# Sixteen copies of the conv tap rows in DRAM for the read of the conv band

## Chip, cores and metric

One core of one Trainium2 chip. The metric is the device time of one execution in microseconds (us).

## What is computed

A causal convolution over the sequence with one softmaxed 7-tap filter per head, followed by a two-layer feed-forward block. Cut to what matters:

```python
# x (8, 4096, 192), weight (8, 7), w_in (192, 2048), w_out (2048, 192), all float32
w = softmax(weight, axis=-1)                       # 8 heads, 7 taps
x_pad = concatenate([zeros(B, 6, D), x], axis=1)   # causal padding
out = einsum('hk,bskhg->bshg', w, windows of x_pad)  # 24 channels per head
a = out.reshape(32768, 192)
h = a @ w_in
g = where(h > 0, h, exp(min(h, 0)) - 1)            # ELU
result = g @ w_out                                 # (32768, 192) float32
```

## The kernel before

The 32,768 tokens are cut into 32 super-tiles of 1,024 tokens. A super-tile runs through 16 steps, one for each 128 columns of the hidden layer; steps are numbered n = 0 to 511 over the whole kernel. In each step TensorE (PE) makes the hidden values H of two groups of 512 tokens (`w_in` matmuls, L748), ScalarE (ACT) takes their exponential E (L542), GpSimd (POOL) clips it to at most 1 (L470), VectorE (DVE) combines E and H into the ELU output gT (L609), and PE later multiplies gT with `w_out` into ops (L782), which ACT evicts to osb and SyncE (SP) stores. PE's whole order is written out at build time in the list `steps`; PE works through it in order and waits where an operand or a PSUM bank isn't there.

The convolution of super-tile s is done ahead of its feed-forward, on PE: the band matrix Tm (128 partitions, 8 heads, 128 columns, bf16), which holds the taps of each head along its diagonals, is the stationary operand and the x rows in xg the moving one (L726). ACT evicts the result to csb (L520), and a transposing DMA that SP issues turns it into att, the left operand of the `w_in` matmuls. Super-tile 0 takes another way, through xT and diagonal matrices Dg, so the first matmuls with Tm are those for super-tile 1. `EARLY_CONV` puts them beside steps n = 7 to 10, and those of super-tile 2 at n = 13 and 14. Ahead of its first one, PE waits in this order for the band, for the x rows, and for their zero padding:

```python
if m == 0:
    W(s_band, 48)
...
for part in range(2):
    x_ready(W, s, part)
```

How Tm is made: SP issues three DMAs, all on its own queue, after the small weight load and one load of x rows (xf). The first (L799) writes zero rows from the zeroed tile zw to the DRAM tensor conv_taps, the second (L804) writes the eight heads' tap rows from zt (128 elements each, the softmaxed taps at columns 6 to 12), and the third (L809) reads the band back. Before the second SP waits for zt (`W(s_wp, 1)`), before the third for both writes (`W(s_band, 32)`). In conv_taps a copy of the taps is ten rows of 128: a zero row, eight heads, a zero row. Partition p of Tm reads eight rows' worth of elements from a start that moves one element back per partition, so each partition gets the taps shifted by one: 1,024 elements, 2,048 bytes, in one run. With two copies, the outer dimension of that read is 2 and the next one 64.

Beside these, POOL issues the big loads of the beginning, one after the other, each with a cast from float32: the six pieces of `w_in` (L424), the two halves of xg for super-tile 1 (L397), `w_out` (L454) and the two halves of xg for super-tile 2 (L397). They all move through the same DMA engines as SP's transfers. SP's next issue after the band is the first transpose.

Of the kernel before, what the change touches and what calls it, by code (L numbers as in the profile page):

```python
# [8 lines left out]
BF16 = mybir.dt.bfloat16  # L9
# [3 lines left out]
P = 128  # L13
HP = 64
FC = 128
D = 192
HEADS = 8
KSIZE = 7
CPH = 24
CW = 128  # L20
# [4 lines left out]
TAP = 6  # L25
# [16 lines left out]
CONV_AT = ((0, 1, 1, 0), (4, 1, 1, 1), (9, 2, 0, 0), (12, 2, 0, 1))  # L42
EARLY_CONV = ((7, 1, 0, 0), (8, 1, 0, 1), (9, 1, 1, 0), (10, 1, 1, 1), (13, 2, 0, 0), (14, 2, 0, 1))
OPS_CONV = 2
FIRST = {}
M_NS, R_NS, C_NS = 215.8, 82.5, 102.5
QUAD = 4
# [6 lines left out]
def bass_lightweight_conv__then__act_elu_kernel(  # L54
# [28 lines left out]
    def take_bank(what):  # L83
        k = len(prior)
        prior.append(occupant[k % 6])
        occupant[k % 6] = what
        turn_of[what] = k % 6
# [4 lines left out]
    for t in range(NS):  # L92
        for half, stretches in enumerate(ROUNDS):
            n, at = NQ * (t + 1) + LAG + 8 * half, [0, 0]
            if t == 0 and half in FIRST:
                n, stretches = FIRST[half]
            for turned, sizes in stretches:
# [35 lines left out]
    def acc_of(op):  # L133
        t, half, q, kb, turned = op[1]
        return (t, half, kb if (t, half) == (last, 1) else 0, op[3])
# [48 lines left out]
    for x_, op in enumerate(steps):  # L184
        if op[0] in "hc" and not any(op[3:]):
            if op[0] == "h" or op[1] >= OPS_CONV:
                take_bank(op[:3])
# [27 lines left out]
            t, half = divmod(n_half - 1, 2)  # L215
            previous[n_half // 2, n_half % 2, 0, g] = (t, half, 0, g)

    taps = nc.dram_tensor("conv_taps", (2 * (HEADS + 2) * CW,), BF16).ap()

    xb = nc.dram_tensor("x_cast", (NT, D), BF16).ap()  # L220

    with ExitStack() as stack:
        def sbuf(name, shape, dt):
            return stack.enter_context(nc.sbuf_tensor(name, shape, dt))
# [28 lines left out]
        zt = sbuf("zt", [HEADS, CW], BF16)  # L253
        xf = sbuf("xf", [P, 2, QUAD, D], FP32)
        zw = sbuf("zw", [P, GS], BF16)
# [76 lines left out]
        def bank_of(what):  # L332
            if what[0] == "c" and what[1] < OPS_CONV:
                return ops[:, what[2], :]
            k = turn_of[what]
            return H[:, k // 2, GS * (k % 2) : GS * (k % 2 + 1)]

        def load_first(eng, k):
            eng.dma_start(
                xf[:, k, :, :].rearrange("p i d -> p (i d)"),  # L340
                x_flat[GS * k : GS * (k + 1), :].rearrange("(p i) d -> p (i d)", i=QUAD),
            ).then_inc(s_xl[k], 16)

        def conv_read(W, m):
            W(s_ce, 2 * (m + 1))

        def out_group(eng, t, half, g, kb=None):
            b = (2 * t + half) % 2
            row = SUP * t + GS * g + 2 * P * half
            if kb is not None:  # L350
                eng.dma_start(
                    out[row + P * kb : row + P * (kb + 1), :], osb[:, b, g, kb, :]
                ).then_inc(s_out[b], 16)
                return
            dst = out[row : row + 2 * P, :].rearrange("(k p) d -> p k d", p=P)
            if t == 0:
                dst = bass.AP(
                    tensor=out.tensor,
                    offset=(GS * half + 1 - g) * D,
                    ap=[[QUAD * D, P], [2 * D, 2], [1, D]],  # L360
                )
            eng.dma_start(dst, osb[:, b, g, :, :]).then_inc(s_out[b], 16)
# [5 lines left out]
        def taken(W, acc):  # L368
            W(s_od if acc in on_dve else s_oev, place[acc] + 1)
# [16 lines left out]
        def turn_att(eng, s):  # L386
            eng.dma_start_transpose(
                out=att[:, s % 2, :, :].rearrange("p j (w t) -> p (j w) t", t=TOK),
                in_=csb[0:TOK, s % 2, :],
            ).then_inc(s_att[s % 2], 16)  # L390
# [228 lines left out]
        def _tensor(pe):  # L619
# [4 lines left out]
            def wait_bank():  # L624
                was = prior[turns[0]]
                turns[0] += 1
                if was is None:
                    return
                if was[0] == "h":
                    W(s_tt, 2 * was[1] + was[2] + 1)  # L630
                else:
                    W(s_ce, 2 * was[1] + was[2] + 1)
# [62 lines left out]
            for x_, op in enumerate(steps):  # L695
# [10 lines left out]
                elif op[0] == "c":  # L706
# [5 lines left out]
                    elif hh == 0:  # L712
# [6 lines left out]
                        W(s_z, z_need[s])  # L719
                        if m >= OPS_CONV:  # L720
                            wait_bank()
# [40 lines left out]
                else:  # L762
# [6 lines left out]
                    if x_ in begins:  # L769
# [4 lines left out]
                        else:  # L774
                            W(s_ce, 2 * (OPS_CONV - 1) + g + 1)
                    elif steps[seen[acc]][2] != rt:
# [16 lines left out]
        @block.sync  # L793
        def _sync(sy):
            W = Waits(sy)
            sy.dma_start(wh[:], weight[:, :]).then_inc(s_wd, 16)
            load_first(sy, 1)
            W(s_zw, 1)
            sy.dma_start(  # L799
                bass.AP(tensor=taps.tensor, offset=0, ap=[[(HEADS + 2) * CW, 2], [(HEADS + 1) * CW, 2], [1, CW]]),  # L800
                zw[0:2, 0 : 2 * CW].rearrange("p (a e) -> p a e", a=2),
            ).then_inc(s_band, 16)
            W(s_wp, 1)
            sy.dma_start(  # L804
                bass.AP(tensor=taps.tensor, offset=CW, ap=[[CW, HEADS], [(HEADS + 2) * CW, 2], [1, CW]]),
                zt[:, :].unsqueeze(1).to_broadcast([HEADS, 2, CW]),
            ).then_inc(s_band, 16)
            W(s_band, 32)
            sy.dma_start(  # L809
                Tm[:, :, :].rearrange("p h e -> p (h e)"),  # L810
                bass.AP(tensor=taps.tensor, offset=CW + TAP + KSIZE - 1, ap=[[(HEADS + 2) * CW - HP, 2], [-1, HP], [1, HEADS * CW]]),
            ).then_inc(s_band, 16)

            def load_cast(s):
                W(s_cv, 4 * (s - NXB))
                W(s_xb[s % 2], 16 * ((s - 1) // 2 + (s % 2)))
                if s > NXB + 1:
                    W(s_xb[(s - 1) % 2], 16 * ((s - 2) // 2 + ((s - 1) % 2)))
                for part in range(2):
                    row = s * SUP + GS * part - PAD  # L820
                    for w0, w1, rows in ((0, WPG - 1, P), (WPG - 1, WPG, GS - TOK * (WPG - 1) + PAD)):
                        v0 = WPG * part
                        sy.dma_start(
                            xg[0:rows, s % NXB, v0 + w0 : v0 + w1, :],
                            bass.AP(
                                tensor=xb.tensor,
                                offset=(row + TOK * w0) * D,
                                ap=[[D, rows], [TOK * D, w1 - w0], [1, D]],
                            ),
                        ).then_inc(s_xq[s % NXB][part], 16)  # L830

            for x_, op in enumerate(steps):
                if op[0] == "h" and op[2:] == (0, 0):
                    s, i = divmod(op[1], NQ)
                    if i == X_LOAD and s and s + 3 < NS:
                        load_cast(s + 3)
                    if op[1] == X_LATE[1]:
                        load_cast(3)
                elif op[0] == "c" and op[3:] == (1, HB - 1):
                    m, b = op[1:3]  # L840
                    s = m // 2 + 1
                    if m % 2 and b:
                        conv_read(W, m)
                        for u in range(2):
                            W(s_h[u], NQ * (s - 1))
                        turn_att(sy, s)
                elif x_ in stops:
                    acc = acc_of(op)
                    t, half, kb, g = acc
                    if (t, half) == (last, 1):  # L850
                        if (kb, g) != (1, 1):
                            taken(W, acc)
                            out_group(sy, t, half, g, kb)
                    else:
                        taken(W, acc)
                        out_group(sy, t, half, g)
            for b in range(2):
                sy.wait_ge(s_out[b], 32 * NS + 32 * b)
# [28 lines left out]
```

## Time and profile before

| what | value |
|---|---|
| median of 3 runs | 730.81 us (730.28 to 730.85) |
| the profiled execution's own time | 730.68 us |
| its span | 728.6 us |
| granted TensorE clock, mean | 0.995 |
| DMA packets | 129,883, 69.12 MB |
| SP's hardware queue (q1) | 123,592 packets, 30.3% of 16 engines' span |
| POOL's software queue (q0) | 5,872 packets, 14.8% |
| band read Tm<-conv_taps | one issue, 256 KB, at 5.68 us |

The span runs from the first to the last instruction of the profiled execution; its own time has some 2 us more around it. Times in the trace count from the span's start. A "wait" names the engine that stood idle, the line it stood before, and what came last. The chain follows the work that ended last backwards, at each step to what released it. The granted clock is the share of TensorE's full speed; 0.50 is half speed.

### The profile page before, as it was taken

To read this page: it belongs to the slowest core of one execution; us is meant where nothing else is said; L and a number is where in the kernel's file an instruction comes from. 1 tells how busy PE (TensorE), PEld (TensorE's weight loads), DVE (VectorE), ACT (ScalarE), POOL (GpSimd) and SP (SyncE) were. 2 spreads that over 40 slices of the span, in tenths; PEclk is the share of its full clock that TensorE was granted. 3 is DMA by queue.
4 is the path that set the end of the run, shared out by engine and by line. 5 is a ranking of instruction groups with operands and counts; after the bars stand their busy time and mean duration, and the time that the engine had idled before them with its cause. 6 is when DMAs were issued, how large, how long until landed. Compare 5 with 4: busy or idle time off the path is not lost.

```text
span 728.6 us, 28723 instructions
## 1 busy us (share of the span) xinstructions
PE 715.9 (98%) x11866; PEld 620.9 (85%) x11866; DVE 651.0 (89%) x1043; ACT 656.0 (90%) x1286; POOL 631.0 (87%) x1078
## 2 busy tenths in 40 slices
PE   8699999999999999999999999999999999999997
PEld 4398888888888888888888888888888888888897
DVE  5599999999999999999999999999999999999994
ACT  6699999999999999999999999999999999999993
POOL 8588888898888898888898888898888898888893
PEclk9899999999999999999999999999999999999999
DMA  9655335455435544335455445355446454532212
GB/s 176 105 102 115 71 93 117 95 91 99 86 95 115 91 94 107 79 93 116 90 95 99 86 95 115 87 99 97 85 97 116 80 105 95 92 93 70 59 35 67
DMA packets 129883, 69.12 MB, mean 95 GB/s; under 512 B 93960, under 2 KB 128520, under 8 KB 129288
## 3 DMA queue, kind: packets, MB, share of 16 engines
q1 hardware_dynamic: 123592, 52.04, 30.3%
q0 software_dynamic: 5872, 14.75, 14.8%
q8 instruction: 93, 1.52, 0.9%
q10 hardware_dynamic: 288, 0.49, 0.2%
q14 instruction: 38, 0.31, 0.1%
HBM read 43.51 MB, written 36.58 MB: 110 GB/s over the span
## 4 chain that ended last, share of the span: by engine, by line
PE 95%; DMA 2%; POOL 1%; ACT 0%; DVE 0%; issue 0%; ACTq 0%
PE ops L782 51%; PE H L748 40%; PE H L726 3%; DMA xg<-in_x_dram 2%; PE H L782 1%; POOL w_in L424 1%; POOL E L470 0%; DVE gT L609 0%; ACT E L542 0%; PE ops L726 0%; POOL xg L397 0%; ACT csb L520 0%; POOL x_cast L413 0%; POOL x_cast L416 0%; POOL sel L439 0%
## 5 line engine op out<-in xcount | busy, mean ns | idle before, releaser
L609 DVE SCALAR_TENSOR_TENSOR gT<-E,H 128x512 f16<-128x512 f32 x1024 | 645.2, 682 | 63.3 <-POOL E L470 56.0
L470 POOL TENSOR_SCALAR E<-E 128x512 f32<-128x512 f32 x1024 | 606.1, 616 | 85.2 <-ACT E L542 81.1
L542 ACT ACTIVATE E<-H 128x512 f32<-128x512 f32 x1024 | 565.0, 611 | 55.5 <-PE H L748 50.7
L748 PE MATMUL H<-att,w_in 64*128 64x512 bf16 x3072 | 604.9, 378 | 1.3 <-DVE gT L609 1.1
L782 PE MATMUL ops<-w_out,gT 64*128 64x192 f16 x8064 | 587.0, 243 | 0.0
L782 PEld LDWEIGHTS ops<-w_out,gT 64*128 64x128 f16 x8064 | 516.4, 94 | 54.5 <-PE ops L782 29.4
L748 PEld LDWEIGHTS H<-att,w_in 64*128 64x128 bf16 x3072 | 258.9, 94 | 20.8 <-DVE gT L609 6.5
L726 PE MATMUL H<-xg,Tm 64*128 64x240 bf16 x480 | 87.6, 263 | 0.3 <-DVE gT L609 0.3
L520 ACT ACTIVATE csb<-H 128x480 bf16<-128x480 f32 x120 | 70.7, 589 | 0.0
L512 ACT ACTIVATE osb<-ops 128x384 f32<-128x384 f32 x125 | 61.0, 488 | 7.3 <-PE ops L782 5.7
L726 PEld LDWEIGHTS H<-xg,Tm 64*128 64x128 bf16 x480 | 38.2, 93 | 16.2 <-issue 0.6
L416 POOL DMA_DIRECT2D x_cast<-in_x_dram x29 | 15.6, 538 | 0.0
L726 PE MATMUL ops<-xg,Tm 64*128 64x240 bf16 x16 | 4.3, 362 | 5.4 <-DMA xg<-in_x_dram 5.4
L726 PEld LDWEIGHTS ops<-xg,Tm 64*128 64x128 bf16 x16 | 1.6, 114 | 7.3 <-issue 5.9
L782 PE MATMUL H<-w_out,gT 64*128 64x192 f16 x128 | 6.4, 243 | 0.0
L782 PEld LDWEIGHTS H<-w_out,gT 64*128 64x128 f16 x128 | 5.7, 94 | 0.0
L637 PE MATMUL ops<-zw 128*128 128x512 bf16 x9 | 3.6, 579 | 1.3 <-DVE zw L552 1.3
L601 DVE COPY osb<-ops 128x384 f32<-128x384 f32 x1 | 0.6, 558 | 4.3 <-PE ops L782 4.3
L698 PE MATMUL ops<-zw 64*128 64x512 bf16 x12 | 4.4, 377 | 0.0
L424 POOL DMA_DIRECT2D w_in<-in_moe_w_in_dram x6 | 3.9, 662 | 0.2 <-DMA wh<-in_weight_dram 0.2
L637 PEld LDWEIGHTS ops<-zw 128*128 128x128 bf16 x9 | 1.2, 141 | 3.2 <-issue 1.9
L397 POOL DMA_DIRECT2D xg<-in_x_dram x4 | 3.5, 878 | 0.0
(49 smaller groups left out, 28.0 us busy)
## 6 DMA issues: line engine op xcount, KB each, us to landing
out_dram<-osb SPq DMA_DIRECT2D x126, 192.0 KB, 3.3
x_cast<-in_x_dram POOLq DMA_DIRECT2D x29, 384.0 KB, 5.3
xg<-x_cast SPq DMA_DIRECT2D x58, 192.0 KB
xg<-x_cast SPq DMA_DIRECT2D x58, 26.2 KB
xg<-in_x_dram POOLq DMA_DIRECT2D x4, 240.0 KB, 17.6
w_in<-in_moe_w_in_dram POOLq DMA_DIRECT2D x2, 384.0 KB, 9.9
w_out<-in_moe_w_out_dram POOLq DMA_DIRECT2D x1, 768.0 KB, 18.9
w_in<-in_moe_w_in_dram POOLq DMA_DIRECT2D x2, 288.0 KB, 6.4
```

Source lines behind the costliest of these rows:

```text
L416: g.dma_start(xb[s * SUP : (s + 1) * SUP, :].rearrange("(p t) d -> p (t d)", p=P), x_flat[s * SUP : (s + 1) * SUP, :].rearrange("(p t) d - ...
L424: g.dma_start(w_in[HP * r : HP * (r + 1), :, c0:c1], moe_w_in.rearrange("(p j) f -> p j f", j=3)[:, :, c0:c1],).then_inc(s_w[k], 16)
L470: g.tensor_scalar(out=E[:, n % NE, u, :], in0=E[:, n % NE, u, :], scalar1=1.0, scalar2=0.0, op0=ALU.min, op1=ALU.max,).then_inc(s_clp)
L512: a.activation(*out_pieces(acc), ACT.Copy).then_inc(s_oev)
L520: return a.activation(csb[:, s % 2, :].rearrange("p (j v h i) -> p h j v i", j=3, v=2 * WPG, h=HEADS)[:, h0 : h0 + HB], bank_of(("c", m, b ...
L542: a.activation(E[:, n % NE, u, :], bank_of(op[:3]), ACT.Exp).then_inc(s_exp)
L609: v.scalar_tensor_tensor(out=gT[:, s % NG3, q, u, :], in0=E[:, n % NE, u, :], scalar=1.0, in1=bank_of(op[:3]), op0=ALU.subtract, op1=ALU.m ...
L637: pe.matmul(ops[:, 0, :], zw[:, 0:P], zw[:], start=True, stop=True)
L698: pe.matmul(ops[:, 1 - rt, :], zw[HP * rt : HP * (rt + 1), 0:P], zw[HP * rt : HP * (rt + 1), :], start=True, stop=True, tile_position=(HP ...
L726: ins = pe.matmul(bank_of(op[:3])[:, n1 * hh : n1 * (hh + 1)], Tm[HP * rt : HP * (rt + 1), h, :], xg[HP * rt : HP * (rt + 1), s % NXB, :, ...
L748: ins = pe.matmul(bank_of(op[:3]), w_in[HP * r : HP * (r + 1), j, RUN * FC * (q // RUN) + q % RUN : RUN * FC * (q // RUN + 1) : RUN,], att ...
L782: ins = pe.matmul(to[:, d0 : d0 + D], gT[HP * rt : HP * (rt + 1), t % NG3, q, g, t0 : t0 + P], w_out[HP * rt : HP * (rt + 1), q, :], start ...
```

## The change

conv_taps gets sixteen copies of the ten rows instead of two. The zero write covers sixteen copies (from sixteen partitions of zw), the tap write repeats each head's row sixteen times, and the band read's outer dimension becomes 16 with 8 partitions each. The elements that each partition of Tm receives are the same.

```diff
+BANDS = 16
...
-    taps = nc.dram_tensor("conv_taps", (2 * (HEADS + 2) * CW,), BF16).ap()
+    taps = nc.dram_tensor("conv_taps", (BANDS * (HEADS + 2) * CW,), BF16).ap()
...
             sy.dma_start(
-                bass.AP(tensor=taps.tensor, offset=0, ap=[[(HEADS + 2) * CW, 2], [(HEADS + 1) * CW, 2], [1, CW]]),
-                zw[0:2, 0 : 2 * CW].rearrange("p (a e) -> p a e", a=2),
+                bass.AP(tensor=taps.tensor, offset=0, ap=[[(HEADS + 2) * CW, BANDS], [(HEADS + 1) * CW, 2], [1, CW]]),
+                zw[0:BANDS, 0 : 2 * CW].rearrange("p (a e) -> p a e", a=2),
             ).then_inc(s_band, 16)
             W(s_wp, 1)
             sy.dma_start(
-                bass.AP(tensor=taps.tensor, offset=CW, ap=[[CW, HEADS], [(HEADS + 2) * CW, 2], [1, CW]]),
-                zt[:, :].unsqueeze(1).to_broadcast([HEADS, 2, CW]),
+                bass.AP(tensor=taps.tensor, offset=CW, ap=[[CW, HEADS], [(HEADS + 2) * CW, BANDS], [1, CW]]),
+                zt[:, :].unsqueeze(1).to_broadcast([HEADS, BANDS, CW]),
             ).then_inc(s_band, 16)
             W(s_band, 32)
             sy.dma_start(
                 Tm[:, :, :].rearrange("p h e -> p (h e)"),
-                bass.AP(tensor=taps.tensor, offset=CW + TAP + KSIZE - 1, ap=[[(HEADS + 2) * CW - HP, 2], [-1, HP], [1, HEADS * CW]]),
+                bass.AP(tensor=taps.tensor, offset=CW + TAP + KSIZE - 1, ap=[[(HEADS + 2) * CW - P // BANDS, BANDS], [-1, P // BANDS], [1, HEADS * CW]]),
             ).then_inc(s_band, 16)
```

## The prediction

> **What bounds the kernel now.** I read the page's engine rows first, then the TensorE waits of the stage around the conv band, then the chain, then stretches of that stage, then the trace's landing records of the DMAs involved.
>
> The page first. PE is busy 98% of the span and the chain that ended last is 95% PE:
>
> ```profile
> PE 715.9 (98%) x11866; PEld 620.9 (85%) x11866; DVE 651.0 (89%) x1043; ACT 656.0 (90%) x1286; POOL 631.0 (87%) x1078
> PE 95%; DMA 2%; POOL 1%; ACT 0%; DVE 0%; issue 0%; ACTq 0%
> ```
>
> So PE leaves 728.6 - 715.9 = 12.7 us idle in all, and a few DMA transfers can only matter inside that. The DMA share of the chain, 2%, is one piece. The waits between 17 and 30 us, longest first (engine, line, waited-for: total, times, longest), and the chain in order of time (start, us, what):
>
> ```profile
> POOL E L470 <- ACT E L542: 7.2, 3, 5.9
> ACT E L542 <- PE H L748: 6.8, 3, 6.1
> DVE gT L609 <- POOL E L470: 6.7, 3, 5.6
> PEld ops L726 <- issue: 5.9, 2, 5.6
> PE ops L726 <- DMA xg<-in_x_dram: 5.4, 1, 5.4
> ```
> ```profile
> 7.29 15.86 DMA xg<-in_x_dram
> 23.15 0.14 issue
> 23.28 0.35 PE ops L726
> ```
>
> The reader is to see one stall. At step n = 7 PE reaches the first conv matmul (L726). It waits 5.36 us, until 23.28; ACT, POOL and DVE run dry behind it. The last thing to come was the second half of the x rows of super-tile 1 (an xg load that POOL issued at 7.29 and that landed at 23.15). From 40 us on PE has no idle at all, so what is saved up to there should reach the end.
>
> Now the stage in stretches (columns: busy PE, PEld, DVE, ACT, POOL, then granted clock, DMA share, GB/s):
>
> ```profile
> 17.90:21.30 3.40, 0.03 (x1) 0.00 (x0) 2.57 (x5) 0.78 (x2) 1.59 (x3) 1.00 1.34 215
> 21.30:23.30 2.00, 0.02 (x2) 0.05 (x3) 0.00 (x0) 0.00 (x0) 0.00 (x0) 0.51 1.45 177
> 23.30:28.20 4.90, 4.84 (x30) 2.79 (x30) 1.46 (x3) 3.06 (x6) 2.02 (x4) 0.50 0.26 35
> 28.20:32.60 4.40, 3.61 (x27) 1.25 (x24) 3.70 (x7) 4.28 (x10) 3.42 (x7) 1.00 0.04 5
> ```
>
> The DMA engines are saturated during the wait, and the clock is at half (0.50) for 4.9 us after it: the stall is paid twice.
>
> Why does that xg load land so late? By the landing records, fourteen of its sixteen increments came between 16.67 and 18.39 us (mean 17.32), the other two at 22.74 and 23.15. The earlier half shows the same: fourteen by 17.09, two at 21.30 and 21.75. The band's read (Tm from conv_taps, L809, issued at 5.68) has just two data landings, at 21.55 and 22.02, and its 128 packets of 2,048 B run from 11.06 to 21.5 us as two interleaved trains. **Two DMA engines carry the whole band, and the x rows that share these two engines come 4 to 5 us after the rest.** Even without the xg wait, the band itself would hold PE until 22.02.
>
> **What the Trainium skill says.** "DMA: Bandwidth & Descriptors", section "Why a DMA increments its semaphore by 16 and not by 1": an SP-issued DMA runs on the largest k up to 16 that divides the slowest dimension of both sides; only those k engines post a landing and the sequencer writes the other 16 - k. The trace agrees: the band's semaphore shows three early increments (2.13, 4.07, 6.76, each some 0.4 to 1.1 us after an issue), ten landings (5.00 to 5.66: two for the zero rows, eight for the tap rows) and the last two of the read. Same page, section "Queues, rings and completion order": an engine serves its queues in turn, a packet each. The trace agrees from 11.06 us on, when a band packet comes every 0.245 us on each of the two engines beside w_in packets and later every 0.12 us beside xg packets; it doesn't show it for the 5.4 us between the issue and the first packet, in which only earlier POOL transfers ran. "TensorE: Matmul & The Clock Gate", section "Part 1: The HAM clock gate (the "warmup" mystery)": the clock halves after a wholly idle window of about 3.4 us. The trace agrees: half clock from 21.35, 3.43 us after PE's last matmul ended (17.92), until 28.18.
>
> **The change part by part.** No engine's instruction list changes: the same three SP DMAs, the same order, the same waits.
>
> (a) *Band read.* k goes from 2 to 16, so 8 packets on each engine instead of 64 on two. Price of one band packet to the xg load behind it: (22.95 - 17.32) / 64 = 88 ns (mean of the two late landings less the mean of the fourteen). So the two engines lose 5.6 us of load and all sixteen get 8 x 0.088 = 0.70 us. The slowest of the fourteen now sets the xg landing: 18.39 + 0.70 = 19.09.
>
> (b) *Tap rows.* Still eight engines (eight head rows outermost), but 16 packets of 256 B each instead of 2. At 18 to 31 ns (the durations in the trace), 14 more cost 0.25 to 0.43 us; if each also waits for one w_in packet (66 to 79 ns in the trace), 1.2 to 1.5. On the xg load I charge 0.30 (pure occupancy; bounds 0 and 0.43, since packets in between belong to loads that must run anyway): 19.39. It also delays SP, which waits for these landings before it issues the band: 5.68 becomes 6.0 to 7.2. Behind that SP wait stand only out stores and transposes, the first at 31.38, so nothing else is late.
>
> (c) *Zero rows.* Two packets on each of sixteen engines instead of two; the landings come near 5.0 as before, since they follow the x loads on SP's queue. Before (b) in time: nothing; without that cover, 2 x 31 ns.
>
> (d) *When does the band land?* With the 5.4 us from issue to first packet as before, it starts at 11.4 to 12.6, and eight packets at the 0.245 us spacing take 2.0 us: about 14, well before 19.4. A bound from above: queued wholly behind both xg halves it would land with them, near 19.4. The w_in pieces may move by up to 0.4 us; the last wait on one (0.5 us at 11.7, n = 2) sits ahead of 1.5 us of slack at n = 7.
>
> (e) *Restart.* PE started 0.13 after the landing, so 19.39 + 0.13 = 19.52 instead of 23.28: **3.76 us**. From the mean landing plus 0.70 to the slowest plus 1.2 the restart lies between 18.2 and 19.8, the gain between 3.5 and 5.1.
>
> (f) *Clock.* PE idles from 17.92 to 19.5, 1.6 us, so no window of 3.4 us is empty and the clock stays full. At half clock the first exponentials (E, L542) of n = 7, 8, 9, 10 began at 24.73, 26.69, 28.36 and 29.79. Only the last gap, 1.43 us, is ACT's own pace (two E's and one conv eviction csb, with overlaps). At full clock I take 0.8 instead of 1.45 us to the first E (half, and a little latency), then three steps of 1.43: 5.09 us instead of 29.79 - 23.28 = 6.51. **1.42 us**; 1.0 to 1.6 while the clock holds (a first E at 1.2 or at 0.6 us), 0 if it falls all the same.
>
> (g) *What is late next.* w_out (fourteen landings by 22.29) and the xg rows of super-tile 2 (fourteen by 24.82) also lose their two stragglers, at 27.00 and 29.59 now. With the same 1.0 us added they come at 23.3 and 25.8; they are needed where PE used them at 32.77 and 32.53, less 5.2: 27.6 and 27.3. So they hold nothing, with 1.5 us to spare. After that ACT, then PE, set the pace as before.
>
> Sum: 3.76 + 1.42 = 5.2 us off the profiled execution's own 730.68 (span 728.6 and 2.08 around it), which is 0.13 under the median 730.81. So 725.5 there and **725.6** as a median.
>
> **Rivals.**
> R1, restart early but the clock term fails (the clock halves in spite of the short idle, or POOL and DVE set n = 7 to 10): 730.81 - 3.76 = 727.0. For it: TensorE's activity in that window is only half. Against: the only falls in the trace, 21.35 and 727.9, follow full windows with no matmul.
> R2, the band becomes the last to land. If the start of its packets is held up with the later issue, all sixteen engines wait with it, and a landing at 21 to 22 leaves 1 to 2 us: 729.0. For it: 5.4 us to the first packet, which I can only carry over. Against: only eight packets an engine.
> R3, the split isn't what makes the two engines late (two engines slow by themselves, or HBM the limit): 730.8. Against: the stragglers show only in loads that run beside the band; w_in's first landings at 5 to 6 us have none of 4 us.
> R4, slower: the sixteen-fold tap write. If its 128 small DRAM writes drain so slowly that SP issues the band after POOL has issued its last load (10.8 us, 5.1 us later than now), the band queues behind w_out and the xg rows of super-tile 2 (last fourteen at 24.8 plus 1.0) and PE restarts near 26: +2.7 us at the old clock, 733.5. It decides from a tap landing of some 10 us on, where I expect 6 to 7.2.
>
> **How the numbers follow.** Forecast 0.68, R1 0.16, R2 0.10, R3 0.03, R4 0.03. The forecast's own bounds: 3.5 + 1.0 to 5.1 + 1.4 us off the median, 724.3 to 726.3. The range takes R1 in, and of R2 the better part: 724.3 to 727.9. About 0.2% (1.5 us) is what a measurement of this kernel can tell from no change; forecast, R1 and most of R2 lie beyond it: faster 0.94, same 0.03, slower 0.03.
>
> **What would show it.** Right: the idle before the first L726 falls from 5.4 to about 1.6 us and the chain still names xg; the xg landings have no pair of stragglers; sixteen band landings by 15 us or so; no 0.50 clock before the end; PE first meets L726 near 19.5. Wrong: a band landing after xg's, half clock after 21 us, a new wait on w_out or on the next xg rows near 27 us, or stragglers that stay.

## The result and the profile after

The changed kernel takes 725.96 us (median of 4, 724.59 to 727.43) against 730.83 us before (730.28 to 730.86): ratio 0.9935, 95% interval 0.9915 to 0.9956, or 4.9 us less. In two more sets of five the ratio was 0.9928 (0.9916 to 0.9941) and 0.9940 (0.9927 to 0.9954). The profiled execution, with 724.59 us and a span of 722.5, is the fastest of the fourteen in these three sets, so its trace shows the gain at its largest.

Of the page, PE's busy row and the shares of the chain:

```profile
PE 714.7 (99%) x11866; PEld 620.3 (86%) x11866; DVE 651.1 (90%) x1043; ACT 655.9 (91%) x1286; POOL 631.0 (87%) x1078
PE 95%; DMA 2%; POOL 1%; ACT 1%; issue 0%; DVE 0%; ACTq 0%
```

PE now leaves 722.5 - 714.7 = 7.8 us idle instead of 12.7. The waits between 17 and 30 us (total, times, longest), then the chain (start, us), with "..." for lines left out:

```profile
POOL E L471 <- ACT E L543: 1.5, 5, 0.5
PEld ops L727 <- ACT csb L521: 1.5, 2, 0.8
ACT E L543 <- PE H L749: 1.0, 2, 0.6
...
PE ops L727 <- DMA xg<-in_x_dram: 0.5, 1, 0.5
```
```profile
7.29 11.57 DMA xg<-in_x_dram
...
19.00 0.26 PE ops L727
```

The same wait has shrunk from 5.4 to 0.5 us. The chain still names xg, now landing at 18.86. The stretches of the stage (busy PE, PEld, DVE, ACT, POOL, then clock, DMA share, GB/s):

```profile
17.90:19.50 1.60, 1.07 (x11) 0.50 (x10) 1.60 (x4) 1.08 (x2) 1.60 (x4) 1.00 1.36 204
19.50:21.30 1.80, 1.57 (x17) 0.66 (x14) 1.64 (x4) 1.46 (x4) 1.31 (x3) 1.00 1.32 203
21.30:23.30 2.00, 1.45 (x15) 0.82 (x16) 1.84 (x4) 2.00 (x6) 1.60 (x3) 1.00 1.52 192
23.30:28.20 4.90, 4.31 (x44) 2.12 (x43) 4.43 (x8) 4.88 (x12) 4.29 (x8) 1.00 0.74 94
```

There is no half clock, and from 21.3 to 28.2 us ACT is busy almost without a break (6.88 of 6.90 us; with the half clock before, 3.06 of the 4.90 us to 28.2): it sets the pace of n = 7 to 10. By the landing records all sixteen xg increments come between 17.18 and 18.86 (mean 18.14) with no pair left behind, and the band has sixteen landings between 13.89 and 16.04.

Where the 6.1 us between the two spans come from, by the starts of DVE's gT instructions matched one by one: n = 0 to 6 run 0.53 us *later* than before; n = 9 is 5.64 us earlier; then the lead stays between 5.64 and 5.67 us for the remaining 500 steps. The last 0.43 us is in SP's closing stores.

### The profile page after: what moved, and what is told of

It is laid out like the page before. It is cut to its first block, busy times and chain, and to the rows that moved or that the text cites. A ratio compares the mean times of both kernels' runs of the same rounds, so it can differ in the third digit from the quotient of the medians.

```text
span 722.5 us, 28723 instructions
## 1 busy us (share of the span) xinstructions
PE 714.7 (99%) x11866; PEld 620.3 (86%) x11866; DVE 651.1 (90%) x1043; ACT 655.9 (91%) x1286; POOL 631.0 (87%) x1078
## 4 chain that ended last, share of the span: by engine, by line
PE 95%; DMA 2%; POOL 1%; ACT 1%; issue 0%; DVE 0%; ACTq 0%
PE ops L783 51%; PE H L749 40%; PE H L727 3%; DMA xg<-in_x_dram 2%; PE H L783 1%; POOL w_in L425 1%; POOL E L471 1%; ACT E L543 0%; DVE gT L610 0%; POOL xg L398 0%; ACT csb L521 0%; POOL x_cast L414 0%; POOL x_cast L417 0%; POOL sel L440 0%; ACT osb L513 0%
```

## Experiments

**How much does the number of engines matter? Four and eight copies.**

```diff
-BANDS = 16
+BANDS = 4      # bands4; 8 in bands8
```

> Four copies instead of sixteen: the band read on four engines, 32 packets each. My theory (each band packet costs the xg load on its engine 88 ns): twelve xg landings by some 18.5 us and four late ones at 17.3 + 2.8 = 20.0 to 20.5; first conv matmul at 20.2 to 20.6, clock full, time 726.5 to 727.2. Rival (what matters is the number of copies in DRAM or anything but the share of an engine): no group of four; the time is that of sixteen copies or of two, 726.0 or 730.8.

> Eight copies: the band read on eight engines, 16 packets each. My theory: eight engines get 1.4 us more, 17.3 + 1.4 = 18.7, which is about where the slowest engine without any band packet stands (18.4), so landings end by 18.7 to 19.3, and the time is that of sixteen copies within 0.5 us: 725.5 to 726.5. Rival (the whole of the gain needs sixteen engines): between four and sixteen copies by a clear step, over 726.8.

bands4 took 728.45 us (ratio 0.9968, 0.9956 to 0.9981), bands8 726.69 (0.9942, 0.9928 to 0.9955). The piece of xg in the chain of each (start, us), first four copies, then eight:

```profile
7.50 13.47 DMA xg<-in_x_dram
```
```profile
7.60 13.29 DMA xg<-in_x_dram
```

Both land near 20.9. The band itself lands in four and in eight increments, so the outer dimension sets the number of its engines here too. By xg's landings, four copies show four late increments (19.90 to 20.97, mean 20.29) behind twelve of mean 17.71: 2.58 us for 32 packets, 81 ns each, near the 88 ns that the prediction took from the kernel before (5.62 us for 64). In that kernel's trace a band packet itself lasts 84 to 96 ns. The 81 ns is an upper reading, since the latest four of sixteen trail in any case: with sixteen copies, where every engine carries the same share, they do so by 0.88, 1.17 and 1.65 us in the three profiles.

With eight copies a group of eight can't be told from the usual spread. The later half of the landings (mean 19.76) trails the earlier (18.35) by 1.41 us, but with sixteen copies it trails by 0.87 to 1.34 us too. So the lag grows with the band packets on an engine, shown for two and for four copies. The times fall in the same order, 730.69, 728.45, 726.69 and 725.39 us with two, four, eight and sixteen (the intervals of the last two overlap), and the rival that any number of copies would do is out.

Both times are later than I expected. The mean of all sixteen landings wasn't the same in each execution: 18.03 before, 18.35 with four copies, 19.05 with eight, 18.14 with sixteen; what moves it is not shown. With four copies the clock, which I expected to stay full, was also at half from 22.44 to 25.85 us, so that from the first conv matmul (21.11) to n = 10 it took 5.52 us instead of 5.07.

**The writes without the read.**

```diff
 # as changed, but the band is read as before
-... ap=[[(HEADS + 2) * CW - P // BANDS, BANDS], [-1, P // BANDS], [1, HEADS * CW]] ...
+... ap=[[(HEADS + 2) * CW - HP, 2], [-1, HP], [1, HEADS * CW]] ...
```

> Sixteen copies written, the band read from two of them as before (two engines, 64 packets each): the change's writes without its read. My theory: the writes cost the xg load at most 0.4 us and delay the band's issue from 5.7 to some 6.4 us, and the two late landings stay at 22.7 to 23.6: 730.7 us, between 730.3 and 731.3. Rival (spreading the rows over DRAM, not over the engines, is what helps): 726. Rival (the writes cost the changed kernel something that its read makes up for): over 731.5.

730.68 us, ratio 0.9999 (0.9991 to 1.0008): the sixteen-fold write costs nothing that shows, and having the rows at sixteen places in DRAM brings nothing while the read takes two of them. Its chain has the old piece back,

```profile
7.39 15.49 DMA xg<-in_x_dram
...
23.02 0.35 PE ops L727
```

and the two stragglers land at 22.87 and 22.88. The whole effect is the read's. Whether reading from sixteen places instead of two helps by itself, apart from the engines, no run separates; against it, the late loads read other tensors, and as many of their landings are late as the band has of its own, two.

**The clock by itself.** Dummies keep PE busy through the old stall.

```diff
 if m == 0:
+    if b == 0:
+        warm(20)       # in the kernel before
     W(s_band, 48)
```

> The kernel before with 20 matmuls on zeroes (128x512) that PE runs just ahead of its wait for the band and xg, so that it is busy to about 22.3 us; nothing else changes, and what they write is overwritten. My theory: xg still lands at 23.15 and conv starts at 23.3, but the clock stays full, and n = 7 to 10 take 5.1 instead of 6.5 us: 730.8 - 1.4 = 729.4 us (729.2 to 729.7). Rival (ACT, POOL and DVE set the pace of these steps whatever the clock): 730.8. Rival (the dummies hold PE up): slower than 730.8.

728.46 us, ratio 0.9972 (0.9962 to 0.9981). ACT's instructions from the restart on (start, us, group, idle before):

```profile
24.16 1.09 ACT L542 ACTIVATE E<-H 128x512 f32<-128x512 f32 x2 [4.93 <-PE H L750]
25.13 0.58 ACT L520 ACTIVATE csb<-ops 128x480 bf16<-128x480 f32 x1
25.58 1.11 ACT L542 ACTIVATE E<-H 128x512 f32<-128x512 f32 x2
26.53 0.62 ACT L520 ACTIVATE csb<-ops 128x480 bf16<-128x480 f32 x1
26.98 1.15 ACT L542 ACTIVATE E<-H 128x512 f32<-128x512 f32 x2
27.93 0.66 ACT L520 ACTIVATE csb<-ops 128x480 bf16<-128x480 f32 x1
28.38 1.19 ACT L542 ACTIVATE E<-H 128x512 f32<-128x512 f32 x2
```

The restart is where it was, at 23.32, but n = 10 begins at 28.38: 5.06 us after it instead of 6.50, and the lead of DVE's gT instructions over the kernel before settles at 1.3 us. So the half clock after the stall cost 1.3 to 1.4 us, separately from the stall; the pace of 1.40 us per step is ACT's. The time fell by 2.0 to 2.2 us, more than that. The surplus in this profile is the end: the second of SP's last two full stores was issued in 0.48 us where the kernel before took 1.62. The issues that contain it, before, after and here (start, us; the second number covers both issues where it says x2):

```profile
723.31 2.04 SPq L362 DMA_DIRECT2D out_dram<-osb  x2
```
```profile
718.07 1.13 SPq L363 DMA_DIRECT2D out_dram<-osb  x1
```
```profile
722.02 0.90 SPq L362 DMA_DIRECT2D out_dram<-osb  x2
```

From the last matmul's start to the last landing it is 3.90, 3.47 and 2.90 us. What makes that issue long is not settled, nor whether it is short in the other executions of this kernel.

**The prediction's slower rival, set up on purpose.**

```diff
 W(s_band, 32)
+W(s_w[1], 32)          # in the changed kernel, ahead of the band read
```

> The changed kernel, but SP also waits for the second part of w_in (landed at 11.8) before it issues the band read, by when POOL has issued all its loads (last at 10.8). This puts the prediction's slower rival at its own deciding point. Rival of the prediction (the band queues behind everything that POOL has issued, w_out and the xg rows of super-tile 2 too): the band lands near 26, the first conv matmul waits for it, 733 us or so. Turn by turn at once: it lands by 15 us, 725.4. My theory, in between: the first packet comes about 5 us after the issue, as at 5.7 (11.06) and at 6.4 (11.20), so at 16.8, and eight packets at 0.12 to 0.25 us end by 17.8 to 18.8: the restart stays with xg or is level with it, 725.4 to 726.5.

725.58 us, ratio 0.993 (0.9917 to 0.9943). The band was issued at 11.91, after POOL's last load; its first packet came at 15.95 and all sixteen landings between 17.36 and 18.45, ahead of xg (19.10). So a band issued that late does not queue behind w_out and the xg rows of super-tile 2, and the rival's deciding point of 10 us doesn't hold. The time from issue to first packet was 5.4 us before, 4.8 after and 4.0 here. A wait behind work already handed to the engines would fit, but what fills this stretch is not shown.

**Another order of POOL's loads, in both kernels.**

```diff
-load_w_in(2, (0, 1))
 load_x(1, 0)
 load_x(1, 1)
+load_w_in(2, (0, 1))
```

> The same order of POOL's loads in the kernel before (two copies, band on two engines). My theory: the band itself is the next to hold PE: it lands near 21.5 to 22.1, xg on the two engines earlier than that or about then, so the first conv matmul starts near 22.1 instead of 23.3, and the last w_in pieces, late on the same two engines (near 22 to 23), hold n = 8: 729 to 730.7. Rival (the order of the loads was the fault, not the band's two engines): as good as the changed kernel, 726 or less.

> The changed kernel with POOL issuing the two halves of xg for super-tile 1 ahead of the last two pieces of w_in (needed one step later, at n = 8). My theory: xg lands about 3 us earlier (15 to 16.5), so n = 7 starts without a wait at some 18.0 to 18.5; the last w_in pieces land where xg did, 18.3 to 20.3, and n = 8 waits for them up to 1 us; in all 0.5 to 2 us less than the changed kernel: 724.0 to 725.0. Rival (w_in's late pieces now hold n = 8 just as long): 725.4, as the changed kernel. Rival (ACT, POOL and DVE are behind anyway): the same, with no PE wait to be seen.

With two copies: 729.86 us, ratio 0.9989 (0.9982 to 0.9996). PE's waits in order:

```profile
21.30 0.38 PE L726 MATMUL ops<-xg,Tm 64*128 64x240 bf16 x1 [2.84 <-DMA Tm<-conv_taps]
24.47 0.60 PE L748 MATMUL H<-att,w_in 64*128 64x512 bf16 x1 [1.31 <-DMA w_in<-in_moe_w_in_dram]
```

The band itself now holds PE, and the w_in pieces that share its two engines (24.20 and 24.42) hold it again one step later. The fault of the kernel before is thus the two engines and not the order: in either order the load that PE needs next is late on them. With sixteen copies: 724.97 us, ratio 0.9922 (0.9909 to 0.9935), and the wait has moved to w_in at n = 8:

```profile
20.69 0.39 PE L749 MATMUL H<-att,w_in 64*128 64x512 bf16 x1 [1.49 <-DMA w_in<-in_moe_w_in_dram]
```

Its median is the lowest of all, but its interval overlaps those of the changed kernel: not shown to be better. That n = 8 would wait for w_in was expected, up to 1 us; it is 1.5. The bytes that must arrive by n = 8 are the same in either order.

**Why do the runs spread more than before?**

> The changed kernel once more. My theory: the restart at n = 7 is set by the slowest of the sixteen xg landings, and the little idle ahead of it no longer swallows what the start of the kernel does (in the first profile n = 0 to 6 ran 0.53 us later than before, with the full clock granted from 6.99 instead of 4.29 us, and the idle ahead of the first conv matmul was 0.53 instead of 5.36). So the runs should keep spreading over 2 to 3 us (724.5 to 727.5, median 725.5 to 726.3), and a second profile should show the xg landings between 17.2 and 19.2, without two stragglers, and n = 9 onwards earlier than before by 4.8 to 5.7 us. Rival (the spread was chance): all runs within 0.6 us as those before, at 724.6 or at 726.

725.39 us (724.80 to 727.15). The profiled execution is the slowest of the five and differs from the first profile twice. One engine lands xg at 20.30, 0.9 us after the one before it, so PE restarts at 20.43. And the clock halves:

```profile
19.50:21.30 1.80, 0.87 (x10) 0.55 (x10) 1.06 (x2) 0.03 (x1) 0.09 (x1) 0.95 1.32 204
21.30:23.30 2.00, 1.95 (x12) 1.03 (x12) 0.70 (x2) 1.62 (x4) 1.19 (x2) 0.50 1.47 195
```

The step to n = 10 takes 5.79 us instead of 5.07. DVE's lead settles at 3.57 us instead of 5.65.

To separate the two, five dummies (1.1 us) in the changed kernel, beside the changed kernel on the same chip:

```diff
+            if b == 0:
+                warm(5)        # in the changed kernel
```

> The changed kernel with 5 matmuls on zeroes (128x512, 1.1 us) ahead of PE's wait for band and xg; what they write is overwritten. In the second profile of the changed kernel the clock halved for one window of 3.4 us although PE had worked 1.0 us in the window before, and that cost some 0.65 us; in the first it did not halve. Theory A (this halving, in some executions only, is a good part of the spread): no half clock in the profile but at the end, no execution over 726.7, median 725.0 to 725.4. Theory B (the spread comes from the xg landing and from the last stores): spread and median as without the dummies, 725.4 to 725.6, or up to 0.5 more where the dummies end after xg has landed.

> The changed kernel a third time, on the same chip as the one with dummies. Both theories: median 725.3 to 725.9. A: where the profile shows a half clock between 17 and 25 us, the steps to n = 10 take 0.5 to 0.8 us more from the restart than the 5.1 us at full clock. B: the restart (18.9 to 20.5) and the second-last store's issue on SP (0.5 to 1.7 us) account for the rest.

With dummies 725.11 us (724.91 to 726.73; ratio 0.9932, 0.9919 to 0.9944), without 726.01 (725.85 to 726.68; 0.9940, 0.9927 to 0.9954). The intervals overlap, and an execution with dummies at 726.73 speaks against theory A in its strict form: whether the dummies gain anything is inconclusive. The mean clock of each execution says more. Of the fourteen of the changed kernel only three have 0.997 or 0.998 (726.21, 727.15 and 726.68 us; the last two are profiled, and their traces have one window at half clock between 15 and 25 us). The other eleven, at 0.999 or 1.0, still run from 724.59 to 727.43. So this halving is a part of the spread and not most of it. The third profile showed another part. There PE waited for w_in at n = 2 (the last two increments of that load came at 13.37 and 13.85, where the first profile's last came at 11.77):

```profile
13.90 0.39 PE L749 MATMUL H<-att,w_in 64*128 64x512 bf16 x1 [1.98 <-DMA w_in<-in_moe_w_in_dram]
```

The clock was at half from 15.2 to 18.6 us, and xg landed at 20.88, its last two increments at least 1.05 us behind the other fourteen. In the kernel before, the 5 us of idle ahead of L726 hid the late n = 0 to 6 (by 0.53 us in the profile after, by 0.55 in that with 20 dummies); with 0.5 to 2.4 us left, such delays can reach the end (argued from the idle, not tested). What makes single engines late in one execution and not in another stays open.

## Why the prediction was right, point by point

**The stall and its cause** (two engines carry the band): shown. With two and four copies as many landings trail as the band has engines, by 88 and at most 81 ns a packet, and write16_read2 takes the whole gain away.

**(a) to (e), the restart**, 19.52 forecast: 19.00, 20.43 and 21.02 in the three profiles of the changed kernel. The mean landing was forecast at 17.32 + 0.70 + 0.30 = 18.32; the three profiles have 18.14, 18.64 and 18.74. The weak term is the slowest landing over the mean, taken as 1.07 us from one execution; it was 0.72, 1.66 and 2.14. Twice the restart went beyond the 18.2 to 19.8 given for it: one profile can't give a spread.

**(b), the writes**, 0.30 charged on xg: no cost visible, within 0.1% of the time. Their effect on the band's issue was right: 6.36, 6.35 and 6.00 against 6.0 to 7.2. One figure of the working was misread: 66 to 79 ns isn't what a w_in packet takes in the trace before, where they last 59 to 60 ns in the first two pieces and 134 to 173 in most of the later ones. It served only for the delay of the tap rows, and the band's issue stayed in its range all the same.

**(d), the band's landing**, "about 14": the last came at 16.04. The start at 11.20 was earlier than the range, but the landings trail the last packets (14.41) by up to 1.6 us, which I had not charged. In the other two profiles the last landing came at 17.65 and 16.17. It was still ahead of xg each time, so nothing hung on it.

**(f), the clock**, 1.42 us: 6.50 - 5.07 = 1.43 in the first profile and 1.44 with the dummies alone. The size was right; the condition was wrong. I wrote that the clock stays full as long as no window is empty. It halved after windows in which PE worked, see the last section, so that R1 (the clock fails to hold) comes true in some executions: 0.7 of the 1.4 us was lost in the second profile, and in the third the clock halved too, but ahead of the restart.

**(g), what is late next**: right. Neither w_out nor the next xg rows held PE in the changed kernel (no such wait between 17 and 30 us); in the other load order the next xg rows held it for the first time, for 0.3 us.

**The sum**: forecast 5.2 us; the medians of the three sets fell by 4.6 to 5.3 us. The first profile's 6.1 is restart 4.28 + steps 1.43 - 0.06 lost on DVE + 0.43 at the last stores; the last term was in no step of the prediction. The spans of the other two profiles are 3.5 and 4.0 us under the one before, with the restart 2.85 and 2.26 us earlier. So that the medians meet 5.2 is in part luck: restarts earlier and later than forecast, a clock that sometimes halves and a term at the end that wasn't forecast come out near it. R3 is out, since four landings trail with four copies and the gain goes with the read; R4 by band_late; R2 (the band is last) happened nowhere with sixteen copies, and with two copies as soon as xg was moved out of the way.

## What to carry to other kernels

A DMA whose outermost dimension is small can cost more than its own time: here it made the loads that shared its two engines 4 to 5 us late, and the wait showed the innocent transfer's name. Look at the spread of a transfer's sixteen landings: a group that clearly trails is the signature, and its lag divided by the packets is the price; compare it with the spread that the landings have without the suspect. When a long stall goes, expect the delays ahead of it, and the variation from run to run, to come out into the time.

## What the runs showed of the hardware

- The TensorE clock does not need an empty window to halve. The shorter stretches between its changes are 3.41, 6.83, 10.24, 13.65 and 17.07 us in the traces, one to five times 3.41, so windows of 3.41 us are set off from these changes here. By PE's busy share in a window at full clock, the next was at half after 0% (before), 19% (write16_read2), 29% (after_again), 37% (bands4, before_xg_first) and 42% (after_third), and stayed full after 47% (bands8), 52% (after_xg_first) and 61% (band_late). No window of the twelve profiles goes against this, those near the end included; between 42 and 47% there is none. The two nearest, each with the window behind it (PE's busy time first, clock third from the end):

```profile
11.74:15.15 3.41, 1.43 (x14) 0.60 (x14) 2.48 (x4) 1.58 (x4) 2.16 (x4) 1.00 1.09 230
15.16:18.57 3.41, 3.41 (x18) 1.21 (x16) 2.48 (x4) 2.72 (x6) 2.63 (x5) 0.50 1.45 195
```
```profile
19.31:22.72 3.41, 1.62 (x18) 1.00 (x20) 1.54 (x3) 0.86 (x2) 0.74 (x2) 1.00 1.37 201
22.72:26.13 3.41, 2.67 (x29) 1.22 (x25) 2.62 (x5) 3.41 (x9) 2.91 (x6) 1.00 1.01 124
```

  The Trainium skill's "TensorE: Matmul & The Clock Gate", section "Part 1: The HAM clock gate (the "warmup" mystery)", speaks of an idle window in its table of the two states; here the measurement decides.
- At the restart, a busy share of 43% at half clock (before; 42% in write16_read2, 54% in before_xg_first) left the clock at half for one more window, so that before, a stall of 5.4 us was followed by 4.9 us at half speed.
- One store's issue on SP near the end took 0.48 (before_warm), 1.13 (after) or 1.62 us (before) in kernels that don't differ there, and from the last matmul's start to the last landing it took 2.90, 3.47 and 3.90 us with them.
